# Padding a router's thin bf16 weights to 128 columns, and gating three token tiles at once

## The chip, the cores and the metric

The kernel runs on one core of one Trainium2 chip. The metric is the device time of the whole program in microseconds (us), as the median over runs.

## The reference, cut to what matters

Attention with random features gives 2304 token rows of 512. An MLP with a nonlinearity follows, and then a routed MLP with eight experts, in which the pairs of token and expert are taken in order of falling logit, and every expert takes 288 tokens.

```python
def _moe_ref(x, w_in, w_out):                  # 2304x512, 512x2048, 2048x512
    h = x @ w_in
    return (h - np.tanh(h)) @ w_out

def _moe2_ref(x, w_gate, w1, w2):              # w_gate 512x8, w1 8x512x1024, w2 8x1024x512
    cap = N // E                               # 288
    logits = x @ w_gate
    order = np.argsort(-logits.flatten())
    assigned = -np.ones(N); counts = np.zeros(E)
    for idx in order:
        tok, e = idx // E, idx % E
        if assigned[tok] >= 0 or counts[e] >= cap:
            continue
        assigned[tok] = e; counts[e] += 1
    for e in range(E):
        mask = assigned == e
        out[mask] = np.maximum(x[mask] @ w1[e], 0.0) @ w2[e]
```

## The kernel before, in words

Every operation is handed to a planner (`Plan`): it holds the operation's engine or engines, a planned duration, a due time (`plan.at` plus `lag`) and the buffers that it reads and writes. `Plan.run` deals out all operations in order of planned time and writes each engine's instructions in that order, which is fixed from then on. Loads and stores are issued by the SP queue (SyncE), also in a fixed order; a load whose buffer is not free holds everything behind it. A changed duration, buffer count or operation can shift the order of the operations after it.

The MLP works on six blocks (`j`) of 384 tokens, three tiles of 128 each. High and low parts of each operand are multiplied apart, three products for each pair (lines 603 to 605 for the first matrix, line 650 for the second). Blocks 0 to 3 end in `out_ops` and `gate_ops`, for each tile `t`: the output tile `xm` is transposed (line 672), copied into the buffer `mT`, of which there is one, and multiplied by `wg`, the gate's weights (line 676: the tile stands as 128 weight columns, `wg` moves with 8 columns, plain fp32, four products that appear as eight records). The logits go into `lg`. Blocks 4 and 5 run side by side and have their logits from `last_logits`. While they run, `low_ops` loads the first weight rows of the experts through the ring `dw` of four buffers (line 580), makes their low parts and stores them (line 587).

Then the experts are served one after another. For each expert but the last, `search_ops` finds the threshold logit digit by digit in seven steps. A step compares all logits with up to 32 thresholds on VectorE (`r_cmp`, line 1068), and counts on TensorE (line 1074): the stationary operand is `A2`, a bf16 tile of 18 token tiles x 32 columns of which 8 are in use, taken as 40 columns that span two token tiles, nine products for a step. VectorE turns the counts into a digit (`r_odd`, `r_cond`), TensorE spreads the digit to all partitions (line 1099, a bf16 operand of 128 columns), and VectorE makes the next thresholds. `route_ops` ranks the chosen tokens (lines 1163, 1164) and settles the capacities left (lines 1194 and 1195, weights of 8 columns). `place_ops` finds each slot's token in 18 products with weights of 32 columns (line 1231). `expert_ops` gathers the tokens and multiplies them with the expert's weights (lines 1380 to 1382 and 1399 to 1401, 288 tokens moving). The routing of the next experts stands among these products in TensorE's order.

`length_ops` (line 356) sums squares with bf16 weights of 128 columns and one moving column; it is not changed. `proj` (line 429) multiplies on two halves of the array's rows, plain fp32.

Of the kernel before, what the change touches and what calls it, by code (L numbers as in the profile page):

```python
# [8 lines left out]
F32 = mybir.dt.float32  # L9
F32R = mybir.dt.float32r  # L10
BF16 = mybir.dt.bfloat16
# [175 lines left out]
def tile_kernel(ctx, tc, q, k, v, omega, w_in, w_out, w_gate, w_gate_t, w1, w2, out, dbg=None):  # L187
# [56 lines left out]
    wg = consts.tile([P, NC, E], F32, name="wg")  # L244
# [51 lines left out]
    mTr = sring(wmid, [P, NC, P], F32, "mT", 1)  # L296
# [11 lines left out]

    bT = Buf(None)
# [355 lines left out]
    def gate_ops(j, t, xm):  # L665
        n = j * TPB + t
        tp, mT, lp = Buf(bank), Buf(mTr), Buf(bank)
        lgb = Buf(None)

        def transposes(e):  # L670
            for c in range(NC):
                nc.tensor.transpose(tp.t[:, c * P:(c + 1) * P], xm.t.bitcast(F32)[:, c * P:(c + 1) * P], ident)
# [5 lines left out]
        plan.op(PE, 0.44, transposes, r=[xm], w=[tp], lag=0.8)  # L678
        plan.op({ACT: 0.48, DVE: 0.6}, 0, lambda e: copy(e, mT.t.rearrange("p c n -> p (c n)"), tp.t), r=[tp], w=[mT],
                lag=1.5)  # L680
        plan.op(PE, 0.86, gate, r=[mT], w=[lp], lag=2.4)
        plan.op(DVE, 0.08, lambda e: nc.vector.tensor_copy(lg[:, n, :], lp.t[:, :E]), r=[lp], w=[lgb], lag=3.5)
# [63 lines left out]
    def mlp_ops(start, step, general=False):  # L746
# [4 lines left out]
        for j in range(NBLK - 1):  # L751
# [28 lines left out]
            if along and e1 == E:  # L780
                vg_split()
            for t in range(TPB):
                plan.at = start[j] + step[j] * NF + LAG2 + 0.7 * t
                xm, _ = out_ops(j, t, acc[t])
                gate_ops(j, t, xm)
# [141 lines left out]
    def r_setup():  # L927
# [20 lines left out]
        z = c.tile([P, n], I32, name="thr0s")  # L948
# [20 lines left out]
        sp = iota("spi", [P, P], [[0, P // LO], [1, LO]])  # L969
# [8 lines left out]
        t["tri"] = c.tile([P, P], BF16, name="tri")  # L978
        nc.vector.tensor_scalar(t["tri"], jp, 0.0, None, op0=OP.is_gt)
        t["ones"] = c.tile([P, P], BF16, name="onesb")  # L980
        nc.vector.memset(t["ones"], 1.0)
        t["one36"] = c.tile([P, 2 * NTT], F32, name="one36")
# [5 lines left out]
        t["mfull"] = c.tile([1, 1], BF16, name="mfull")  # L988
        nc.vector.memset(t["mfull"], -1.0e6)
# [29 lines left out]
    def best_ops(rS, after=()):  # L1019
# [9 lines left out]
        vec(0.22, lambda V: V.tensor_tensor(A2.t[:, :, :E], a.t, wide(am.t, E), op=OP.is_equal), r=[a, am], w=[A2])  # L1029
# [3 lines left out]
    pairs = []  # L1033
# [612 lines left out]
```

## Time and profile before

| | |
|---|---|
| median of 3 runs | 898.56 us (895.24 to 898.88) |
| the profiled execution | 897.55 us, of which 895.7 us lie between its first and its last instruction |
| TensorE, products | busy 863.1 us (96%), 6168 records |
| TensorE, weight loads | busy 768.8 us (86%) |
| VectorE | busy 657.8 us (73%) |
| ScalarE | busy 467.6 us (52%) |
| GpSimd | busy 252.5 us (28%) |
| mean granted TensorE clock | 0.988 of full speed |

Busy time counts an engine as busy from an instruction's start to its end, and instructions of TensorE overlap. [...]

### The profile page before, as it was taken

The page shows a single profiled execution, that of the slowest core. Times are in us where ns is not written, and L with a number is a line of the kernel's source. Part 1 is how long each engine was busy: PE and PEld are TensorE (multiplying, and loading weights), DVE is VectorE, ACT ScalarE, POOL GpSimd, SP SyncE. Part 2 cuts the span into 40 slices and gives each one's busy share as a digit, 9 for nine tenths or more (in the row PEclk, how much of TensorE's full clock was granted, in tenths as well). Part 3 has the DMA queues.
Part 4 walks back from the last instruction along what each step waited for, and adds up shares of the span by engine and source line. Part 5 has one row for each costly group of instructions (what it writes and reads, how often), then busy time and mean ns, then how long its engine had stood idle before and what let it go on. Part 6 is the DMA issues. An engine that isn't in the chain of part 4 may idle for free. (4 is left out here: it accounts for less than half of the span.)

```text
span 895.7 us, 17533 instructions
## 1 busy us (share of the span) xinstructions
PE 863.1 (96%) x6168; PEld 768.8 (86%) x6168; DVE 657.8 (73%) x1931; ACT 467.6 (52%) x1017; POOL 252.5 (28%) x272
## 2 busy tenths in 40 slices
PE   8988999999999999999999998989999999999995
PEld 6877888988989888889989995766999999999995
DVE  4998999777587879887867875445887887885520
ACT  4876564644456554655467771012465456465521
POOL 1122344143442435334520332010222322231211
PEclk8999999999999999999999999999999999999998
DMA  8988878877466665633478855576879878777600
GB/s 237 354 267 281 272 228 273 316 238 221 114 201 193 200 202 176 202 103 119 129 261 296 290 216 164 175 268 181 258 224 269 278 170 270 266 205 272 217 28 27
DMA packets 103789, 193.94 MB, mean 217 GB/s; under 512 B 28305, under 2 KB 42257, under 8 KB 103698
## 3 DMA queue, kind: packets, MB, share of 16 engines
q1 hardware_dynamic: 98034, 173.92, 59.3%
q0 software_dynamic: 5664, 18.88, 8.7%
q8 instruction: 49, 0.80, 0.4%
q14 instruction: 42, 0.34, 0.1%
HBM read 149.64 MB, written 33.69 MB: 205 GB/s over the span
## 5 line engine op out<-in xcount | busy, mean ns | idle before, releaser
L603 PE MATMUL bk<-xH,wi 128*128 128x384 f32 x332 | 118.3, 356 | 1.6 <-DVE xt L502 1.0
L604 PE MATMUL bk<-xL,wi 128*128 128x384 f32 x332 | 111.9, 337 | 0.5 <-DVE xL L305 0.5
L605 PE MATMUL bk<-xH,iL 128*128 128x384 f32 x332 | 112.1, 338 | 0.0
L650 PE MATMUL acc<-wo,gL 128*128 128x512 f32 x282 | 111.7, 396 | 0.0
L709 DVE SCALAR_TENSOR_TENSOR lw<-wf,raw 128x512 f32<-128x512 f32 x128 | 108.1, 844 | 2.2 <-POOL wf L706 1.0
L305 POOL TENSOR_TENSOR gL<-s,gH 128x384 fp32r<-128x384 f32 x51 | 61.0, 1196 | 138.3 <-ACT gH L300 128.9
L650 PE MATMUL acc<-wo,gH 128*128 128x512 f32 x240 | 99.8, 417 | 0.0
L440 ACT ACTIVATE phi<-bk,nm 128x128 f32<-128x128 f32 x272 | 77.0, 381 | 37.2 <-DVE nm L443 37.0
L650 PE MATMUL acc<-oL,gH 128*128 128x512 f32 x240 | 95.0, 396 | 0.3 <-DVE oL L305 0.3
L706 POOL TENSOR_TENSOR wf<-oL,wo 128x512 f32<-128x512 f32 x48 | 65.7, 1369 | 73.7 <-DMA oL<-low_wo 62.4
L300 ACT ACTIVATE gH<-s 128x384 fp32r<-128x384 f32 x80 | 42.1, 526 | 71.4 <-DVE s L630 48.5
L628 DVE SCALAR_TENSOR_TENSOR s<-s,bk 128x384 f32<-128x384 f32 x83 | 45.6, 550 | 37.1 <-ACT s L627 36.8
L603 PEld LDWEIGHTS bk<-xH,wi 128*128 128x128 f32 x332 | 62.9, 190 | 8.4 <-PE bk L482 1.3
L604 PEld LDWEIGHTS bk<-xL,wi 128*128 128x128 f32 x332 | 63.0, 190 | 3.3 <-DVE xL L305 0.7
L650 PEld LDWEIGHTS acc<-wo,gL 128*128 128x128 f32 x282 | 52.9, 188 | 12.6 <-POOL gL L305 0.3
L605 PEld LDWEIGHTS bk<-xH,iL 128*128 128x128 f32 x332 | 62.6, 189 | 0.0
L607 ACT ACTIVATE u<-bk 128x384 f32<-128x384 f32 x80 | 39.2, 489 | 39.8 <-PE bk L605 37.5
L443 DVE TENSOR_REDUCE nm<-bk 128x4 f32<-128x512 f32 (+1 forms) x75 | 46.4, 633 | 15.1 <-PE bk L429 14.1
L630 DVE SCALAR_TENSOR_TENSOR s<-s,u 128x384 f32<-128x384 f32 x80 | 54.6, 682 | 1.2
L650 PEld LDWEIGHTS acc<-wo,gH 128*128 128x128 f32 x240 | 45.2, 188 | 6.6 <-issue 0.2
L650 PEld LDWEIGHTS acc<-oL,gH 128*128 128x128 f32 x240 | 45.2, 188 | 6.5 <-DVE oL L305 1.0
L627 ACT ACTIVATE s<-u,qbias 128x384 f32<-128x384 f32 x80 | 49.2, 616 | 2.7 <-DVE gL L305 1.0
(402 smaller groups left out, 2347.0 us busy)
## 6 DMA issues: line engine op xcount, KB each, us to landing
r_wraw<-in_moe_w_dram SPq DMA_DIRECT2D x50, 512.0 KB, 6.0
iL<-low_wi SPq DMA_DIRECT2D x80, 256.0 KB, 3.3
oL<-low_wo SPq DMA_DIRECT2D x78, 256.0 KB, 2.7
raw<-in_moe_w_in_dram SPq DMA_DIRECT2D x32, 512.0 KB, 5.4
raw<-in_moe_w_out_dram SPq DMA_DIRECT2D x32, 512.0 KB, 4.2
dw<-in_moe_w_dram SPq DMA_DIRECT2D x16, 512.0 KB, 5.7
w1l<-dw SPq DMA_DIRECT2D x16, 512.0 KB, 3.0
s_wraw<-in_moe_w_dram SPq DMA_DIRECT2D x14, 512.0 KB, 5.6
```

The lines of the kernel that those rows point to most:

```text
L305: (nc.gpsimd if e == POOL else nc.vector).tensor_tensor(out, in_, high.bitcast(F32), op=OP.subtract)
L440: nc.scalar.activation(ph.t[:, i0 + i, :], pj.t[:, i * M:(i + 1) * M], AF.Exp, bias=nmx.t[:, i0 + i:i0 + i + 1])
L443: plan.op(DVE, 0.1 + 0.125 * n, lambda e, pj=pj, i0=i0, n=n: V.tensor_reduce(nmx.t[:, i0:i0 + n], pj.t[:, :n * M].rearrange("p (i m) -> p ...
L603: nc.tensor.matmul(ph(), piece(iH, c), xH.t[:, c, :], start=(c == 0), stop=False)
L604: nc.tensor.matmul(ph(), piece(iH, c), xL.t[:, c, :], start=False, stop=False)
L605: nc.tensor.matmul(ph(), piece(iL, c), xH.t[:, c, :], start=False, stop=(c == NC - 1))
L627: plan.op(ACT, 0.52, lambda e: nc.scalar.activation(s.t, ut(), AF.Square, bias=qbias), r=[u], w=[s], lag=2.8)
L628: plan.op(DVE, 0.52, lambda e: V.scalar_tensor_tensor(s.t, s.t, QD, ph(), op0=OP.add, op1=OP.mult), r=[p, s], w=[s], lag=3.4)
L630: plan.op(DVE, 0.65, lambda e: V.scalar_tensor_tensor(s.t, s.t, QC, ut(), op0=OP.mult, op1=OP.mult), r=[u, s], w=[s], lag=4.0)
L650: nc.tensor.matmul(acc[t].t, (gL if k == 2 else gH).t[:, c], (oL if k == 1 else oH).t, start=(f == 0 and k == 0), stop=(f == end and k == ...
L706: plan.op(POOL, 1.45, lambda e: nc.gpsimd.tensor_tensor(w.t, lo.t.bitcast(F32), wo[:, f, :].bitcast(F32), op=OP.add), r=[lo, wbuf["wo", f] ...
L709: x_reads.append(plan.op(DVE, 0.9, lambda e, i=i: nc.vector.scalar_tensor_tensor(scratch.t.bitcast(F32), w.t, 1.0, half(rows[i // 2], i % ...
```

## The change

Weights of the routing's thin products become 128 columns wide. In the counting products, 128 columns of `A2` are taken from column 32 j on, so each product reads the following token tiles too, whose counts land in partitions that nobody reads; `A2` (`pairs`) has two tiles more, which are zero. The placing products do the same with `lid`, which has three more zero tiles. The one-hot row `oh` and the sums `gs` are 128 wide with zeros behind the first eight columns, and `mfull` has 128 rows of which the first alone is not zero. These padded tiles are made once, with memsets on GpSimd.

The gate transposes and copies each tile as before, into an `mT` of 384 columns. Then one burst for the block takes `wg` (32 columns for each quarter of the model dimension, 8 in use, zeros behind) as the weights and the 384 tokens as the moving operand; the four quarters write to four column tiles of the array, 32 partitions each. The result is copied to `lT`, a buffer of the ring `s`, transposed back in three transposes, and VectorE sums the four quarters into `lg`.

To fit in memory, the ring `dw` has three buffers instead of four, and in the setup the tile `spi` takes the place of `jp` after `tri` has been made from it, and a scratch tile that of `one36`. The part of the program that only runs when the values are out of range (not in these runs) shares one more buffer and has other due times.

```diff
-    wg = consts.tile([P, NC, E], F32, name="wg")
+    wg = consts.tile([P, NC, P // NC], F32, name="wg")
-    mTr = sring(wmid, [P, NC, P], F32, "mT", 1)
+    mTr = sring(wmid, [P, NC, BLK], F32, "mT", 1)
...
-    def gate_ops(j, t, xm):
+    def gate_ops(j, xms):
+        mT, lp, lT, lgb = Buf(mTr), Buf(bank), Buf(sr), Buf(None)
+        own = lambda z, w: z.t[:, :TPB * w].rearrange("p (t n) -> p t n", t=TPB)
+        for t, xm in enumerate(xms):
+            tp = Buf(bank)
...
+            plan.op(PE, 0.44, transposes, r=[xm], w=[tp], lag=0.8 + 0.7 * t)
+            plan.op({ACT: 0.6, DVE: 0.68}, 0, lambda e, t=t, tp=tp: copy(
+                e, mT.t[:, :, t * P:(t + 1) * P], tp.t.rearrange("p (c n) -> p c n", n=P)), r=[tp], w=[mT], lag=1.5 + 0.7 * t)
         def gate(e):
             for c in range(NC):
-                nc.tensor.matmul(lp.t[:, :E], mT.t[:, c, :], wg[:, c, :], start=(c == 0), stop=(c == NC - 1))
+                nc.tensor.matmul(lp.t[c * P // NC:(c + 1) * P // NC, :BLK], wg[:, c, :], mT.t[:, c, :], start=True, stop=True,
+                                 skip_group_check=True)
+        def back(e):
+            for t in range(TPB):
+                nc.tensor.transpose(own(lp, P)[:, t, :], lT.t[:, t * P:(t + 1) * P], ident)
-        plan.op(PE, 0.86, gate, r=[mT], w=[lp], lag=2.4)
-        plan.op(DVE, 0.08, lambda e: nc.vector.tensor_copy(lg[:, n, :], lp.t[:, :E]), r=[lp], w=[lgb], lag=3.5)
+        plan.op(PE, 0.9, gate, r=[mT, bwg], w=[lp], lag=4.0)
+        plan.op({ACT: 0.48, DVE: 0.55}, 0, lambda e: copy(e, lT.t, lp.t[:, :BLK]), r=[lp], w=[lT], lag=5.0)
+        plan.op(PE, 0.33, back, r=[lT], w=[lp], lag=5.6)
+        plan.op(DVE, 0.25, lambda e: nc.vector.tensor_reduce(
+            lg[:, j * TPB:(j + 1) * TPB, :], own(lp, P).rearrange("p t (c e) -> p t e c", c=NC)[:, :, :E, :], axis=AX.X,
+            op=OP.add), r=[lp], w=[lgb], lag=6.0)
...
-        sp = iota("spi", [P, P], [[0, P // LO], [1, LO]])
+        t["tri"] = c.tile([P, P], BF16, name="tri")
+        nc.vector.tensor_scalar(t["tri"], jp, 0.0, None, op0=OP.is_gt)
+        sp = jp
+        nc.gpsimd.iota(sp, pattern=[[0, P // LO], [1, LO]], base=0, channel_multiplier=0)
...
-            t = wr[0].tile([P, NTT, 32], BF16, name=f"pairs{i}")
+            t = wr[0].tile([P, NTT + 2, 32], BF16, name=f"pairs{i}")
...
+            lids.append(Buf(None, wr[0].tile([P, NTT + 3, 2, LO], BF16, name=f"lid{i}")))
+            plan.op(POOL, 0.1, lambda e, i=i: nc.gpsimd.memset(lids[i].t[:, NTT:], 0.0), w=[lids[i]])
+        for n in ("oh", "gs"):
+            first[n] = Buf(None, wr[0].tile([P, P], BF16, name=n))
+            plan.op(POOL, 0.1, lambda e, n=n: nc.gpsimd.memset(first[n].t, 0.0), w=[first[n]])
...
-                        nc.tensor.matmul(cnt.t[:32 + E, :2 * n].rearrange("p (a n) -> p a n", a=2),
-                                         A2.t[:, j:j + 2].rearrange("p a e -> p (a e)")[:, :32 + E],
+                        nc.tensor.matmul(cnt.t[:, :2 * n].rearrange("p (a n) -> p a n", a=2),
+                                         A2.t[:, j:j + P // 32].rearrange("p a e -> p (a e)"),
                                          cmp.t[:, j - j0:j - j0 + 2, :n], start=(j == 0), stop=(j == NTT - 2))
...
-                nc.tensor.matmul(rp.t[:E, :1], gs.t, rt["ones"][:, :1], start=True, stop=False)
-                nc.tensor.matmul(rp.t[:E, :1], oh.t[0:1, :], rt["mfull"], start=False, stop=True)
+                nc.tensor.matmul(rp.t[:, :1], gs.t, rt["ones"][:, :1], start=True, stop=False)
+                nc.tensor.matmul(rp.t[:, :1], oh.t, rt["mfull"], start=False, stop=True)
...
-                nc.tensor.matmul(pi.t[:2 * LO, :NHI], lid.t[:, j].rearrange("p a l -> p (a l)"), ohh.t[:, j],
+                nc.tensor.matmul(pi.t[:, :NHI], lid.t[:, j:j + P // (2 * LO)].rearrange("p j a l -> p (j a l)"), ohh.t[:, j],
                                  start=(j == 0), stop=(j == NTT - 1))
...
-    plan.op(SP, 0.47, lambda e: nc.sync.dma_start(wg, w_gate.rearrange("(c p) e -> p c e", p=P)))
+    plan.op(POOL, 0.1, lambda e: nc.gpsimd.memset(wg, 0.0), w=[bwg])
+    plan.op(SP, 0.47, lambda e: nc.sync.dma_start(wg[:, :, :E], w_gate.rearrange("(c p) e -> p c e", p=P)), w=[bwg])
...
-        for r, n in zip(d_rings, (4, 2)):
+        for r, n in zip(d_rings, (3, 2)):
```

## Rows read from the trace of the kernel before

**Rows 1.** Busy time by stretch (us; instructions in brackets), clock, DMA share, GB/s.
```profile
core 0: us, PE busy (x) PEld busy (x) DVE busy (x) ACT busy (x) POOL busy (x), PEclk, DMA share, GB/s
200.00:265.00 65.00, 65.00 (x404) 57.87 (x404) 45.30 (x103) 33.48 (x81) 27.37 (x24) 1.00 0.60 176
476.00:548.00 72.00, 68.49 (x375) 60.97 (x375) 57.53 (x92) 48.92 (x98) 23.24 (x20) 0.98 0.68 242
660.00:694.00 34.00, 34.00 (x302) 31.44 (x301) 27.96 (x125) 19.21 (x32) 9.85 (x13) 1.00 0.94 271
```
**Rows 2.** Waits of TensorE from 548 us on: us in total, times, longest.
```profile
PE rp L1099 <- DVE r_cond L1095: 1.7, 3, 0.6
```
**Rows 3.** Timeline of TensorE in an expert phase: start, us, instruction, count.
```profile
647.51 0.29 PE L1382 MATMUL bd<-r_xgH,wi 128*128 128x288 f32 x1
647.73 0.44 PE L1074 MATMUL rp<-r_cmp,pairs 128*40 128x62 bf16 x9
...
648.34 0.30 PE L1381 MATMUL bd<-r_xgL,wi 128*128 128x288 f32 x1
...
648.89 0.29 PE L1401 MATMUL be<-s_hH,s_ewL 128*128 128x288 f32 x1
649.02 0.18 PE L1099 MATMUL rp<-id,d 128*128 128x8 bf16 x1
...
649.29 0.29 PE L1400 MATMUL be<-s_hL,wi 128*128 128x288 f32 x1
```
**Rows 4.** All counting and all digit products: duration min/median/max in ns, first and last start.
```profile
L1074 PE MATMUL rp<-r_cmp,pairs x441: 176/193/207, 550.1 to 793.3; 128*40 128x62 bf16 x84, 128*40 128x30 bf16 x42, 128*40 128x32 bf16 x21
L1099 PE MATMUL rp<-id,d x49: 166/180/183, 552.0 to 794.7; 128*128 128x8 bf16 x49
```
**Rows 5.** Timeline of TensorE, a count in two pieces.
```profile
555.42 0.29 PE L1074 MATMUL rp<-r_cmp,pairs 128*40 128x62 bf16 x4
```
**Rows 6.** Timeline of TensorE around a place burst.
```profile
672.90 0.30 PE L1382 MATMUL bd<-s_xgH,r_ewL 128*128 128x288 f32 x1
673.13 0.61 PE L1231 MATMUL rp<-r_ohh,r_lid 128*32 128x18 bf16 x18
...
673.91 0.29 PE L1381 MATMUL bd<-s_xgL,s_ewH 128*128 128x288 f32 x1
```
**Rows 7.** Timeline of TensorE around a settling pair.
```profile
667.16 0.29 PE L1382 MATMUL be<-s_xgH,s_ewL 128*128 128x288 f32 x1
667.39 0.17 PE L1194 MATMUL rp<-onesb,r_gs 128*8 128x1 bf16 x1
...
667.81 0.29 PE L1381 MATMUL be<-s_xgL,s_ewH 128*128 128x288 f32 x1
```
**Rows 8.** Timeline of TensorE in the MLP, around four bf16 products of 128 columns.
```profile
249.49 0.34 PE L605 MATMUL bk<-xH,iL 128*128 128x384 f32 x1
249.67 0.25 PE L356 MATMUL bk<-onev,sq 128*128 128x1 bf16 x4
...
250.04 0.34 PE L604 MATMUL bk<-xL,wi 128*128 128x384 f32 x1
```
**Rows 9.** Timeline of TensorE around one tile's gate products.
```profile
166.91 0.34 PE L605 MATMUL bk<-xH,iL 128*128 128x384 f32 x1
167.09 0.95 PE L676 MATMUL bk<-wg,mT 128*128 128x8 f32 x8
...
168.15 0.34 PE L604 MATMUL bk<-xL,wi 128*128 128x384 f32 x1
```
**Rows 10.** Timeline of TensorE: transposes of xm, then products on two row halves.
```profile
265.04 0.60 PE L672 MATMUL bk<-ident,xm 128*128 128x128 f32 x4
265.57 1.16 PE L429 MATMUL bk<-omT,ld 64*128 64x128 f32 x16
266.66 0.50 PE L650 MATMUL acc<-wo,gH 128*128 128x512 f32 x1
```
**Rows 11.** Loads and stores through dw: duration in ns, first and last start.
```profile
L580 SPq DMA_DIRECT2D dw<-in_moe_w_dram x16: 383/428/999, 447.9 to 524.8; - x16
L587 SPq DMA_DIRECT2D w1l<-dw x16: 337/338/423, 459.0 to 540.4; - x16
```

More of the change, by code (lines that the diff above doesn't have):

```diff
@@ L305, in low @@
         (nc.gpsimd if e == POOL else nc.vector).tensor_tensor(out, in_, high.bitcast(F32), op=OP.subtract)
+    bwg = Buf(None)
     bT = Buf(None)
@@ L663, in out_ops, with transposes @@
                            nbytes=P * DM * 4)
-    def gate_ops(j, t, xm):
[L666 to L672, printed above, removed]
+    def gate_ops(j, xms):
[3 more added lines that the diff above has]
+            tp = Buf(bank)
+            def transposes(e, tp=tp, xm=xm):
+                for c in range(NC):
+                    nc.tensor.transpose(tp.t[:, c * P:(c + 1) * P], xm.t.bitcast(F32)[:, c * P:(c + 1) * P], ident)
+            plan.op(PE, 0.44, transposes, r=[xm], w=[tp], lag=0.8 + 0.7 * t)
+            plan.op({ACT: 0.6, DVE: 0.68}, 0, lambda e, t=t, tp=tp: copy(
+                e, mT.t[:, :, t * P:(t + 1) * P], tp.t.rearrange("p (c n) -> p c n", n=P)), r=[tp], w=[mT], lag=1.5 + 0.7 * t)
@@ L781, in mlp_ops @@
                 vg_split()
+            xms = []
             for t in range(TPB):
                 plan.at = start[j] + step[j] * NF + LAG2 + 0.7 * t
-                xm, _ = out_ops(j, t, acc[t])
-                gate_ops(j, t, xm)
+                xms.append(out_ops(j, t, acc[t])[0])
+            plan.at = start[j] + step[j] * NF + LAG2
+            gate_ops(j, xms)
         j, lacc4, lprev4 = NBLK - 2, Buf(bank), None
@@ L947, in r_setup @@
         f0 = c.tile([P, n], I32, name="thr0")
-        z = c.tile([P, n], I32, name="thr0s")
+        t["one36"] = c.tile([P, 2 * NTT], F32, name="one36")
+        z = t["one36"].bitcast(I32)[:, :n]
         nc.vector.tensor_scalar(f0.bitcast(U32), x.bitcast(U32), 0x80000000, None, op0=OP.bitwise_xor)
@@ L987, in r_setup @@
         nc.vector.memset(t["asg"], 0.0)
-        t["mfull"] = c.tile([1, 1], BF16, name="mfull")
-        nc.vector.memset(t["mfull"], -1.0e6)
+        t["mfull"] = c.tile([P, 1], BF16, name="mfull")
+        nc.vector.memset(t["mfull"], 0.0)
+        nc.vector.memset(t["mfull"][:1], -1.0e6)
         t["id8"] = c.tile([P, E], BF16, name="id8")
@@ L1028, in best_ops @@
         vec(0.22, lambda V: V.tensor_reduce(am.t, a.t, axis=AX.X, op=OP.max), r=[a], w=[am])
-        vec(0.22, lambda V: V.tensor_tensor(A2.t[:, :, :E], a.t, wide(am.t, E), op=OP.is_equal), r=[a, am], w=[A2])
+        vec(0.22, lambda V: V.tensor_tensor(A2.t[:, :NTT, :E], a.t, wide(am.t, E), op=OP.is_equal), r=[a, am], w=[A2])
         return m, am, A2
-    pairs = []
+    pairs, lids = [], []
     def pairs_ops():
@@ L1144, in route_ops @@
         if not last:
-            oh, tie = tmp([P, E], BF16, "oh"), tmp([P, NTT], F32, "tie")
-            vec(0.14, lambda V: V.tensor_scalar(oh.t, w.t, mx.t, None, op0=OP.is_equal), r=[w, mx], w=[oh])
+            oh, tie = first["oh"], tmp([P, NTT], F32, "tie")
+            vec(0.14, lambda V: V.tensor_scalar(oh.t[:, :E], w.t, mx.t, None, op0=OP.is_equal), r=[w, mx], w=[oh])
             vec(0.22, lambda V: V.scalar_tensor_tensor(
-                S, oh.t[:, None, :].to_broadcast([P, NTT, E]), -BIG, S, op0=OP.mult, op1=OP.add), r=[oh, rS], w=[rS])
+                S, oh.t[:, None, :E].to_broadcast([P, NTT, E]), -BIG, S, op0=OP.mult, op1=OP.add), r=[oh, rS], w=[rS])
         vec(0.09, lambda V: V.tensor_tensor(av.t, gg.t[:, 1], flat(am.t), op=OP.mult), r=[gg, am], w=[av])
@@ L1181, in route_ops @@
             rp = Buf(rpr)
-            ga, gs = tmp([P, NTT, E], F32, "ga"), tmp([P, E], BF16, "gs")
-            vec(0.22, lambda V: V.tensor_tensor(ga.t, A2.t[:, :, :E], gg.t[:, 1].unsqueeze(2).to_broadcast([P, NTT, E]), op=OP.mult),
+            ga, gs = tmp([P, NTT, E], F32, "ga"), first["gs"]
+            vec(0.22, lambda V: V.tensor_tensor(ga.t, A2.t[:, :NTT, :E], gg.t[:, 1].unsqueeze(2).to_broadcast([P, NTT, E]), op=OP.mult),
                 r=[A2, gg], w=[ga], after=held if not p else later)
```

23 lines of the change are left out of this document (9 added, 14 removed).

## The prediction

> **What bounds the kernel now.** I read the windows by stage first. In the MLP and in the expert phases TensorE is busy for the whole stretch (65.00 of 65.00 and 34.00 of 34.00 us), while VectorE is at 45.3 of 65 and 28.0 of 34; only the stretch with blocks 4 and 5 together leaves 3.5 us of 72 free [rows 1]. The granted clock is 1.00 in two of the three stretches and 0.98 in the other, so the clock is no term of the sum. Busy TensorE is not TensorE at its peak, so the second view was the list of what TensorE waited for from 548 us on: the longest entry is 1.7 us in three waits for the routing's VectorE steps [rows 2]. So TensorE's own order of instructions sets the end almost everywhere, and what a product costs is the distance between starts, not its duration. That is the third view, the timeline of TensorE around single bursts. The reader is to see there how long the normal stream is interrupted.
>
> **The routing's thin products.** Normal pitch of the experts' products (288 moving columns) is 0.13 us (648.89 to 649.02) [rows 3]. I compare two interruptions, each from the last normal product before to the second normal one after, less two pitches (0.26). The digit product (L1099, bf16, 128 weight columns, one product): 649.29 - 648.89 = 0.40, so 0.14. The counting burst (L1074, bf16, 40 weight columns, nine products): 648.34 - 647.51 = 0.83, so 0.57 [rows 3]. Within the burst a product takes (0.44 - 0.193) / 8 = 0.03 [rows 3, 4]. Nine products at the price of the digit product's kind would cost 0.14 + 8 x 0.03 = 0.38. The remaining 0.19 is not work; it stands at the ends (the burst starts 0.22 after the product before it instead of 0.13, and the rest follows its last product). That four 128-wide bf16 products run without it is seen where the weights' squared lengths are summed (L356): 250.04 - 249.49 = 0.55 less two pitches of 0.18, so 0.19 for four, against 0.14 + 3 x 0.03 = 0.23 by the same rule [rows 8].
> The place products (L1231, 32 columns, 18 of them): 1.01 - 0.26 = 0.75 against 0.14 + 17 x 0.026 = 0.58, so 0.17 to gain [rows 6]; the pitch 0.026 is (0.61 - 0.17) / 17. The settling pair (L1194 and L1195, 8 columns): 0.65 - 0.26 = 0.39 against 0.14 + 0.03 = 0.17, so 0.22 [rows 7].
> Counts: 49 steps of the search (one digit product each [rows 4]) with nine counting products each (441). Seven steps come in two pieces, as in [rows 5], so 56 bursts: 56 x 0.2 = 11.2. Eight place bursts: 1.4. Seven settling pairs: 1.5. Together 14.1. In the steps where TensorE waits for VectorE already [rows 2], an earlier count brings nothing behind it; I take off 0.8. **Routing: -13.3 us** (bounds: 0 if width is not the cause; -14.1 as counted; for a gain beyond that every step would have to be in two pieces, which the timeline excludes).
>
> Against the change speaks that three times as many weight columns are loaded. The row to weigh is L356: the group of four lasts 0.25 where a single thin product lasts 0.17 [rows 7, 8], so 128-column loads follow each other by (0.25 - 0.17) / 3 = 0.027. So I cost the wider load at nothing. [...]
>
> **The gate logits.** Now every tile has a burst of eight records (four fp32 products) that costs 168.15 - 166.91 = 1.24 less two pitches of 0.18, so 0.88 [rows 9]; three tiles in a block 2.64, and four blocks have them. Afterwards a block has one burst of four products, 32 weight columns each and 384 moving, and three transposes back. Plain fp32 goes in two records for each product, and 16 records of 128 moving columns on two halves of the array take 1.09 us [rows 10]; less 0.19 for a switch that is 0.90, 0.11 for each pair if two run at once. Four transposes of that width take 0.53, 0.13 each, though each is one record [rows 10]; so two do run at once, and a record of 384 columns takes 3 x 0.11 = 0.33. All four column tiles at once: 2 x 0.33 = 0.66. None at once: 8 x 0.33 = 2.64. I take 1.0, near the lower end because the row halves of [rows 10] overlap, and not at it because one tile's two records are issued ahead of the next tile's. To it come 0.19 for the narrow weights and 0.42 (0.53 - 0.11) for three transposes: 1.61. **Gate: (2.64 - 1.61) x 4 = -4.1 us** (bounds -5.5 and +2.4). [...] The transposes of xm stay. The copies into mT stay too; new is one copy of 128 x 384 for each block on ScalarE or VectorE, and one reduction in place of three small copies. ScalarE has 31 us free of 65 there [rows 1]. They lengthen the way to lg, which the search first needs for its counts at 550 us [rows 4].
>
> **What pays for the memory.** The buffers of the expert weights' low parts (dw) go from four to three. First load to first store takes 459.0 - 447.9 = 11.1 us, and 16 loads to last store 92.5 [rows 11]. Sixteen turns of 11 to 14 us through three buffers take 59 to 75, which fits in 92.5. But a load that must wait for a buffer holds SP's queue, and behind it stand the loads of iL and oL that TensorE needs next. The least is nothing, the most I allow is that the stage's idle TensorE time of 3.5 us [rows 1] doubles. **+1.0** (0 to +3.5).
> The setup's second iota now overwrites jp, so GpSimd waits there for VectorE's tri; behind it on GpSimd stand the low parts gL, which TensorE needs. GpSimd is busy 27 of 65 us [rows 1] and catches up: **+0.3** (0 to +1). The GpSimd memsets of the padding come before the search and take the place of nothing TensorE waits for [rows 2]; the memset of wg stands ahead of its load far before its use: nothing, and at most a few tenths if SP stood behind it. Weights that are read over the neighbour's columns add rows of results that nobody reads. The planner's costs for the routing are the same, so that order stays; the MLP's order is dealt anew, which I allow 2 us either way.
>
> **Sum.** 897.55 (the profiled execution) - 13.3 - 4.1 + 1.0 + 0.3 = 881.5. The median of the runs is 1.0 above that execution; by the median it is 882.5. I say 882.
>
> **Rivals.**
> *Others become late.* When a stretch of 34 us loses seven counts, a place burst and a settling pair (1.8 us), VectorE's 28.0 us are 87% of it, and the DMA share, 0.94 in one phase, rises too [rows 1]. If half of the routing's gain turns into waits for r_cond, r_cmp or weights: 898.6 - 6.7 - 4.1 + 1.3 = 889. Against it: TensorE hardly waits for either today [rows 2]. 0.12.
> *The gate's tiles run one after another,* and the three dw buffers stall SP as well: 898.6 - 13.3 + 2.4 + 1 = 889. 0.05.
> *Width is not the cause.* If what costs 0.19 belongs to these bursts for another reason (say their bursts of accumulation), only the gate's gain is left: 898.6 - 4.1 + 1.3 = 896. Against it: L356 and L1099 are bf16 and accumulate or not, and neither pays it [rows 3, 8]. 0.06.
> *The other side: wide loads do not keep pace in long bursts.* L356 has four in a row; a burst of 9 or 18 could run at the load's own pace. The slowest row with 128-column weights and hardly any moving columns is the gate, 0.88 / 8 = 0.11 for a record [rows 9]. Then 441 x (0.11 - 0.03) + 144 x (0.11 - 0.026) = 47 us come back: 898.6 - 17.4 + 1.3 + 47 = 929. It decides from a pitch of about 0.057 on, where 585 x 0.028 eats the 16. Against it: the gate's weights are fp32, and the four bf16 loads show nothing of it [rows 8]. 0.05. [...]
>
> **How the numbers follow.** The forecast has 0.72. A change of 0.5% (4.5 us) is about what a measurement of this kernel can tell from none, so faster ends at 894. Forecast, late others and serial gate lie below it: 0.72 + 0.12 + 0.05 = 0.89. Width not the cause is the same: 0.06. Slow loads are slower: 0.05. The range goes down to 876 (routing -14.1, gate -5.5, order -2, no cost: 898.6 - 21.6 = 877, and one for the scatter of the runs) and up to 890, which takes in the second and third case. The forecast's own range is 877 to 887.
>
> **What would show it.** Right: counting bursts that start 0.13 after the normal product before them and total about 0.38; each expert's phase shorter by about 1.8 us, so the end moves step by step from 550 us on; gate bursts of about 1 us, four of them; VectorE's busy share up and TensorE's waits still short. Wrong: a pitch inside the counts above 0.05; waits for r_cond in most steps; idle TensorE between 450 and 545 us behind SP's dw loads; a gate burst of 2.5 us.

## The result, and the profile after it

The changed kernel takes 887.11 us (median of 4 runs, 885.15 to 888.42) beside 898.72 (4 runs of the kernel before in the same session, 895.24 to 903.1): a ratio of 0.9865 [0.9839, 0.9892]. It is faster by 11.6 us, 1.3%. The forecast was 16. The profiled execution took 886.79 us, with a span of 884.9 and a mean clock of 0.984.

First the burst that carried most of the forecast. TensorE's timeline of the changed kernel around one counting burst, one settling pair and one place burst (start, us, instruction, count):

```profile
643.20 0.29 PE L1423 MATMUL be<-s_hH,s_ewL 128*128 128x288 f32 x1
643.34 0.44 PE L1096 MATMUL rp<-r_cmp,pairs 128*128 128x62 bf16 x9
643.61 0.38 PE L1421 MATMUL be<-s_hH,s_ewH 128*128 128x288 f32 x1
643.83 0.29 PE L1422 MATMUL be<-s_hL,s_ewH 128*128 128x288 f32 x1
...
661.99 0.29 PE L1404 MATMUL be<-s_xgH,s_ewL 128*128 128x288 f32 x1
662.12 0.18 PE L1216 MATMUL rp<-onesb,gs 128*128 128x1 bf16 x1
...
662.41 0.29 PE L1403 MATMUL be<-s_xgL,s_ewH 128*128 128x288 f32 x1
...
666.61 0.30 PE L1423 MATMUL be<-s_hH,wi 128*128 128x288 f32 x1
666.75 0.61 PE L1253 MATMUL rp<-r_ohh,lid 128*128 128x18 bf16 x18
...
667.43 0.29 PE L1422 MATMUL be<-s_hL,wi 128*128 128x288 f32 x1
```

Read as the prediction read them: from the last normal product before to the second normal one after, less two pitches (0.26). Counts: 643.83 - 643.20 = 0.63, so 0.37 (0.57 before [rows 3], 0.38 forecast). Settling pair: 0.42, so 0.16 (0.39 before [rows 7], 0.17 forecast). Place: 0.82, so 0.56 (0.75 before [rows 6], 0.58 forecast). The burst starts 0.14 after the product ahead of it, no longer 0.22. Each burst got shorter by what was forecast.

The gate's burst in the same timeline, and the three transposes back:

```profile
172.80 0.33 PE L606 MATMUL bk<-xH,iL 128*128 128x384 f32 x1
173.06 0.85 PE L682 MATMUL bk<-mT,wg 128*32 128x384 f32 x8
173.84 0.66 PE L553 MATMUL bk<-ident,xt 128*128 128x128 f32 x4
...
176.40 0.39 PE L651 MATMUL acc<-wo,gL 128*128 128x512 f32 x1
176.63 0.49 PE L687 MATMUL bk<-ident,s 128*128 128x128 f32 x3
176.96 1.04 PE L553 MATMUL bk<-ident,xt 128*128 128x128 f32 x8
```

The eight records of four products start in two groups of four, 0.007 us apart within a group and 0.33 between the groups (173.060, 173.067, 173.073, 173.080, then 173.407 to 173.427), and each record lasts 0.49 to 0.51: all four column tiles run at once. The burst costs 173.84 - 172.80 less one pitch of 0.17, which is 0.87; the transposes 0.33. That is 1.2 for a block where 1.61 was forecast.

Then what TensorE waits for in the changed kernel, first from 530 us on, then within the six phases from expert 1's first product to expert 7's (653 to 847 us) (us in total, times, longest; waits under 0.15 us are not listed):

```profile
PE acc L651 <- SPq L1530: 3.9, 1, 3.9
PE bd L1369 <- DMA r_xg<-ms,r_ix: 2.7, 2, 1.9
PE rp L1121 <- DVE r_cond L1117: 2.6, 3, 1.4
...
PE rp L1121 <- DVE r_cond L1117: 1.4, 1, 1.4
PE be L1364 <- DMA r_xg<-ms,r_ig: 1.3, 2, 1.1
PE be L1364 <- DMA xg_rest<-ms,r_ig: 0.7, 2, 0.6
PE rp L1253 <- DVE r_ohh L1247: 0.4, 1, 0.4
```

Before, the longest waits from 548 us on were three for r_cond, 1.7 us together [rows 2], and the same view of the six phases (662 to 858 us) had no entry at all. So waits have appeared that were not there. The windows by stage (us, busy time of PE, PEld, DVE, ACT and POOL with instructions, clock, DMA share, GB/s) show the same:

```profile
476.00:548.00 72.00, 66.34 (x355) 57.84 (x354) 52.27 (x92) 43.99 (x88) 23.50 (x25) 0.93 0.69 240
532.00:548.00 16.00, 10.50 (x44) 7.54 (x43) 5.74 (x23) 1.89 (x4) 2.53 (x8) 0.68 0.52 182
660.00:694.00 34.00, 34.00 (x322) 32.42 (x321) 28.26 (x134) 18.50 (x31) 9.09 (x12) 1.00 0.84 245
694.00:728.00 34.00, 32.28 (x307) 30.44 (x307) 27.49 (x128) 17.75 (x29) 9.71 (x12) 1.00 0.81 233
```

One phase is full as before [rows 1], the next is short of 1.7 us, and the stretch with blocks 4 and 5 now holds 5.7 us of idle TensorE and a granted clock of 0.93. The largest single wait is at the branch that separates the MLP from the experts (L1530), where TensorE waits for SP's queue for 3.93 us and GpSimd for 8.81. TensorE and SP around it:

```profile
534.70 0.47 PE L651 MATMUL acc<-wo,wi 128*128 128x512 f32 x1 [1.33 <-PEq L1530]
539.09 0.79 PE L651 MATMUL acc<-xm,wi 128*128 128x512 f32 x1 [3.93 <-SPq L1530]
539.68 0.63 PE L651 MATMUL acc<-wo,gLk 128*128 128x512 f32 x1
540.11 0.63 PE L651 MATMUL acc<-wo,wi 128*128 128x512 f32 x1
```
```profile
535.05 0.34 SPq L588 DMA_DIRECT2D w1l<-dw  x1
539.93 0.34 SPq L855 DMA_DIRECT2D gL<-g4l  x1
```

SP reaches the branch only after its last store from dw, at 535.05, and TensorE gets on 4.04 us later. After that idle time its products start 0.43 apart instead of 0.23: the granted clock is 0.50 of full speed from 535.1 to 545.3 us (0.53 in the window from 535 to 536 us, 0.50 from 536 to 545, 0.85 from 545 to 546).

Five stretches, each taken from the first product of its stage, show where the time went in the kernels of this study (us, worked out from one profiled execution of each; "gate" runs from block 0's first product to block 4's, "blocks 4, 5" to the first of the MLP's last products, which stand around the branch, "branch" to the first count, "expert 0" to expert 1's first product, "experts" to expert 7's; the rest is 38.4 to 38.8 everywhere). Two borders need care. "Gate" holds the gate bursts of three blocks; the fourth's stand behind block 4's first product. And the wait at the branch falls into "branch" in most kernels, but into "blocks 4, 5" in e6_store_act, e7_both and e9_e1_ties, while the border of e2_dw3_only lies 1.9 us ahead of its branch; so these two columns are best read as a sum. The order column is explained with the experiments.

| kernel | order | gate | blocks 4, 5 | branch | expert 0 | experts |
|---|---|---|---|---|---|---|
| before | 1 | 388.8 | 103.9 | 4.5 | 112.2 | 195.0 |
| after | 2 | 384.6 | 97.8 | 9.3 | 109.1 | 193.4 |
| e1_routing_only | 3 | 388.5 | 104.0 | 4.4 | 109.8 | 188.1 |
| e2_dw3_only | 4 | 389.6 | 95.8 | 12.2 | 114.4 | 195.0 |
| e3_gate_only | 2 | 382.9 | 97.8 | 9.0 | 111.1 | 198.9 |
| e4_dw_early | 2 | 384.9 | 97.8 | 8.8 | 108.2 | 194.1 |
| e5_order | 1 | 385.3 | 97.7 | 9.3 | 113.3 | 192.2 |
| e6_store_act | 2 | 385.6 | 99.6 | 4.3 | 110.2 | 197.1 |
| e7_both | 1 | 383.3 | 99.6 | 4.5 | 111.6 | 191.5 |
| e8_counts96 | 2 | 385.6 | 97.8 | 8.8 | 111.7 | 197.3 |
| e9_e1_ties | 3 | 385.8 | 99.7 | 4.5 | 110.9 | 188.4 |
| e10_before_ties | 2 | 389.3 | 104.1 | 4.5 | 111.1 | 197.5 |
| e11_after_e1_ties | 3 | 383.4 | 97.8 | 8.9 | 110.1 | 189.4 |
| e12_counts64 | 2 | 384.5 | 97.7 | 9.4 | 115.0 | 198.1 |

The time ahead of block 0 lies between 50.7 and 55.1 us without regard to the kernel; it is scatter. The experiments ran in three sessions, in which the kernel before took 896.79 (e1 to e4), 900.8 (e5 to e8) and 898.89 us (e9 to e12), so ratios are to be compared, and times only within a session.

### The profile page after: what moved, and what is told of

Read it like the earlier page. It is cut to its first block, busy times and chain, and to the rows that moved or that the text cites. A ratio compares the mean times of both kernels' runs of the same rounds, so it can differ in the third digit from the quotient of the medians.

```text
span 884.9 us, 17420 instructions
## 1 busy us (share of the span) xinstructions
PE 846.3 (96%) x6116; PEld 756.0 (85%) x6116; DVE 654.1 (74%) x1925; ACT 470.2 (53%) x1021; POOL 252.9 (29%) x276
## 5 line engine op out<-in xcount | busy, mean ns | idle before, releaser
L305 POOL TENSOR_TENSOR gL<-s,gH 128x384 fp32r<-128x384 f32 x49 | 58.1, 1186 | 138.4 <-ACT gH L300 138.4
L651 PEld LDWEIGHTS acc<-wo,gL 128*128 128x128 f32 x282 | 53.3, 189 | 12.2
L444 DVE TENSOR_REDUCE nm<-bk 128x4 f32<-128x512 f32 (+1 forms) x75 | 46.3, 632 | 12.2 <-PE bk L430 11.1
```

The source lines that it names most:

```text
L305: (nc.gpsimd if e == POOL else nc.vector).tensor_tensor(out, in_, high.bitcast(F32), op=OP.subtract)
L444: plan.op(DVE, 0.1 + 0.125 * n, lambda e, pj=pj, i0=i0, n=n: V.tensor_reduce(nmx.t[:, i0:i0 + n], pj.t[:, :n * M].rearrange("p (i m) -> p ...
L651: nc.tensor.matmul(acc[t].t, (gL if k == 2 else gH).t[:, c], (oL if k == 1 else oH).t, start=(f == 0 and k == 0), stop=(f == end and k == ...
```

## The experiments

**The three parts alone.** The first kernel is the changed one with the gate and the four dw buffers of before; the second is the kernel before with three dw buffers; the third is the changed one with the routing's narrow products of before.

```diff
 e1_routing_only, against the changed kernel
-    def gate_ops(j, xms):
+    def gate_ops(j, t, xm):
...
-        for r, n in zip(d_rings, (3, 2)):
+        for r, n in zip(d_rings, (4, 2)):
 e2_dw3_only, against the kernel before
-        for r, n in zip(d_rings, (4, 2)):
+        for r, n in zip(d_rings, (3, 2)):
 e3_gate_only, against the changed kernel
-                        nc.tensor.matmul(cnt.t[:, :2 * n].rearrange("p (a n) -> p a n", a=2),
-                                         A2.t[:, j:j + P // 32].rearrange("p a e -> p (a e)"),
+                        nc.tensor.matmul(cnt.t[:32 + E, :2 * n].rearrange("p (a n) -> p a n", a=2),
+                                         A2.t[:, j:j + 2].rearrange("p a e -> p (a e)")[:, :32 + E],
...
```

> Only the routing's weights are widened; the gate is that of before and dw has four buffers, so the MLP up to 545 us should be that of before. Theory A (each narrow bf16 burst pays about 0.2 us on TensorE at its ends, 13 us in all, and part of it comes back as waits of TensorE for gathered rows and routing steps of VectorE): about 890 us (887 to 893), bursts of nine counts at 0.34 to 0.38 as in the changed kernel, 6 to 9 us won between 550 us and the end. Rival B (the routing's part is all given back to waits, and the whole gain of the changed kernel is the MLP's, which reaches its end 11 us earlier): 896 to 899 us.

Measured: 0.9909 [0.9879, 0.9939], 888.42 us. Its two stages before the branch stand as before; expert 0 takes 2.4 us less and the experts 6.9 less. The width is the cause of the shorter bursts (0.36 for a burst of nine, as in the changed kernel), and this kernel alone has most of the gain, as theory A expected. It also got an order of its own behind the branch, order 3, in which narrow products were never run; how much of the 6.9 is the order's is not shown.

> The kernel before with three dw buffers instead of four, nothing else. Theory A (with three buffers the last store of the low parts is issued so late that SP reaches the branch after the MLP as the last engine, and TensorE's second product after it waits some 4 us at half clock): 2 to 6 us slower than before, 901 to 905 us, with such a wait near 545 us. Rival B (SP's lateness in the changed kernel comes from its MLP ending earlier than the store stream, whatever the buffers; three buffers cost nothing here): 898 to 900 us.

Measured: 0.9999 [0.9974, 1.0024], 897.32 us. The time stayed, as rival B expected, but not because nothing happened: the wait of theory A is there. Up to the branch, blocks 4 and 5 take 6.2 us less (97.7 beside 103.9), and from the branch to the first count it takes 5.8 us more. TensorE's timeline of this kernel there, and SP's last store:

```profile
542.33 0.47 PE L650 MATMUL acc<-wo,wi 128*128 128x512 f32 x1 [0.57 <-PEq L1507]
547.68 0.79 PE L650 MATMUL acc<-xm,wi 128*128 128x512 f32 x1 [4.88 <-SPq L1507]
```
```profile
543.63 0.34 SPq L587 DMA_DIRECT2D w1l<-dw  x1
```

So the wait comes with the three buffers, but not because they make the stores late. Counted from block 4's first product, the last store goes out after 98.7 us with four buffers and after 99.0 with three (98.1 to 99.0 in all 14 kernels). What moved is TensorE. Before, it reached the branch 5.2 us after the last store (545.60 and 540.38), and nothing was left to wait for; here it is there ahead of the store and gets on 4.05 after it. The time saved ahead of the branch is handed over to the wait. Where the 6.2 come from is not settled: TensorE's same 553 products of that stretch stand in another order here, and its idle time fell from 5.4 to 1.7 us; the granted clock, 0.50 from 463.8 to 467.2 us in the kernel before, is 1.00 in that stretch of the changed kernel (437 to 535 us), which is 6.1 us shorter; no run parts the buffers from the order.

> Only the new gate (with three dw buffers and the setup's shared tiles); the routing's weights stay 40, 32 and 8 columns wide. Theory A (four column tiles at once save 1.3 us for each of four blocks, the end of blocks 4 and 5 waits less, SP's late store takes 4 to 5 us back): 892 to 896 us, with the MLP's end about 11 us earlier as in the changed kernel. Rival B (the MLP's gain is not the gate's but an accident of the order dealt anew together with the routing's operations): MLP end within 4 us of before and 897 to 900 us.

Measured: 0.9997 [0.9965, 1.0028], 895.42 us. The time lies in theory A's range, but only because the kernel before took 896.79 beside it; the ratio shows no gain. In the profiled execution the gate's stage gains 5.9 us and blocks 4 and 5 6.1, and most of it is spent again: 4.5 at the branch and 3.9 among the experts, whose products this kernel doesn't change at all. That last loss was the riddle. Its order of instructions behind the branch is the same as that of the changed kernel, and another than before.

**The wait at the branch.** The loads and stores through dw get earlier due times; or the last two stores go through ScalarE's queue; ScalarE has little to do there (in the changed kernel it is busy 1.89 of the 16 us from 532 to 548 us).

```diff
 e4_dw_early, against the changed kernel
-    low_ops(starts[-2], (NF * steps[-1] + 4.0) / (E * NPRE))
+    low_ops(starts[-2], (NF * steps[-1] - 8.0) / (E * NPRE))
 e6_store_act, against the changed kernel
-            plan.op(SP, 0.47, lambda e, raw=raw, e_=e_, r=r: nc.sync.dma_start(w1l[e_, r, :], raw.t), r=[raw],
-                    nbytes=P * n * 4, lag=6.8)
+            plan.op(SP if k < E * NPRE - 2 else ACT, 0.47, lambda e, raw=raw, e_=e_, r=r: (
+                nc.sync if e == SP else nc.scalar).dma_start(w1l[e_, r, :], raw.t), r=[raw], nbytes=P * n * 4, lag=6.8)
```

> The changed kernel with the due times of the dw loads packed closer, so that the last of 16 is due 11 us earlier. Theory A (the 4.2 us wait of TensorE after the branch and the half clock of 10 us behind it come from the last low-part store on SP): the wait near 535 us shrinks below 1 us and the time falls to 881 to 885 us. Rival B (SP waits there for something else, or the crowd of transfers earlier in blocks 4 and 5 costs as much): 886 to 890 us.

Measured: 0.9895 [0.985, 0.9939], 887.24 us. The wait stayed at 3.93 us, and the last store went out at 536.56, which is 98.1 us after block 4's first product, as in the changed kernel. So the edit did not move the stores at all and decides nothing about the wait; that the planner holds each load back until a store has freed one of the three buffers is the likely reason, not a tested one.

> The changed kernel with the last two stores of low parts issued from ScalarE's queue instead of SP's. Theory A (TensorE's 4.2 us wait after the branch comes from SP, which stands behind the last store and reaches the branch last): the wait falls below 1.5 us, the half-clock stretch behind it gets shorter, 882 to 885 us. Rival B (whoever holds the last store, the branch is late, for instance since ScalarE is now the last): the wait stays and the time is 886 to 889 us.

Measured: 0.9855 [0.9835, 0.9875], 888.09 us. The time is rival B's, and the wait did not fall below 1.5 us: it moved to ScalarE's queue.

```profile
PE acc L651 <- ACTq L1530: 3.1, 1, 3.1
```

But TensorE now gets on 1.5 us after the last store (535.10, then 536.56) and not 4.0, so blocks 4 and 5 and the branch together took 103.9 instead of 107.1; the granted clock from 532 to 548 us was 0.89 instead of 0.68 (by estimate 3.5 us at 0.50 instead of 10.2), and the first count came 3.1 us sooner. What takes the other 2.5 us when SP issues the last store is not shown. Then the experts took 197.1, 3.7 more than in the changed kernel, and the gain was gone. The same order gave 193.4, 194.1 and 197.1 in three kernels with wide products: its waits for gathered rows and VectorE differ, and with one profile of each it is open whether by kernel or by execution.

**The order behind the branch.** The planner gives out operations by the key `(round(t / 0.03), o.prio)`: planned starts that fall into the same step of 0.03 are a tie. At the branch all engines' planned times are set to one value, `now`, and that value depends on the costs of everything before. Apart from a few short memsets on GpSimd the operations behind the branch and their costs are the same in both kernels; `now` differs, so ties round otherwise, and 603 of TensorE's 953 operations there get another place. Adding less than 0.04 to `now` chooses between orders without touching an operation. Four orders appeared: 1 is that of the kernel before, 2 that of the changed kernel, 3 that of e1_routing_only, 4 that of e2_dw3_only. The five kernels that choose an order:

```diff
 e5_order, against the changed kernel (e7_both has the stores of e6_store_act as well)
-    now = max(plan.free.values())
+    now = max(plan.free.values()) + 0.03854
 e11_after_e1_ties, against the changed kernel (e9_e1_ties has the stores of e6_store_act as well)
+    now = max(plan.free.values()) + 0.03669
 e10_before_ties, against the kernel before
+    now = max(plan.free.values()) + 0.02146
```

> The changed kernel with one number added: the planner's clock at the start of the routing stage is moved by 0.03854 us of planned time, so that its ties (times are compared in steps of 0.03) fall as in the run with the routing's weights alone; no operation is changed. Theory A (in the changed kernel the order of routing and experts was dealt anew by those ties, and the new order lets TensorE wait for gathered rows and for VectorE): the stretch from the second to the last expert, 193.4 us now, falls to 187 to 190, and the whole time to 881 to 885 us. Rival B (the waits are what faster TensorE runs into in any order): within 1.5 us of the changed kernel, 885.5 to 888.5 us.

Measured: 0.987 [0.9845, 0.9895], 888.84 us. The order that it writes is not that of e1_routing_only, as was meant, but that of the kernel before, which makes it the better test: it is the order that the prediction counted on. The time is the changed kernel's (0.9865), so theory A's gain did not come. The experts take 192.2, only 2.8 less than with narrow products in the same order, and expert 0 takes 1.1 more. The waits of its TensorE among the experts, where the kernel before has none:

```profile
PE rp L1121 <- DVE r_cond L1117: 3.4, 6, 0.9
```

Here the first rival of the prediction is seen as it was described: with the bursts shorter, VectorE's digit is late in steps where it was in time before.

> Both of the two edits before. Theory A: the two add up, 877 to 881 us. Rival B: neither or one alone, 882 to 888 us.

Measured: 0.9823 [0.9801, 0.9845], 884.44 us, in rival B's range and short of theory A's. Blocks 4 and 5 and the branch together take 104.1 instead of 107.0, and with this order the program keeps that gain.

> The kernel before with the planner's clock at the start of the routing stage moved by 0.02146 us, with which every engine's order behind the branch is exactly that of the changed kernel; no operation is changed. Theory A (the order dealt anew costs some 4 us by itself, as the run with the gate alone, 198.9 us from the second to the last expert against 195.0, suggests): 197.5 to 200 us for this stretch, ratio 1.002 to 1.007. Rival B (the order is worth nothing, the gate's run lost its 3.9 us otherwise): 194 to 196 us, ratio 0.998 to 1.002.

Measured: 1.0008 [0.9985, 1.0032], 900.43 us. With narrow products, order 2 costs the experts 2.4 us and gives expert 0 1.1 back. The experts stand at the lower edge of theory A's range, the ratio in rival B's: in the time of the whole program no loss can be told from none.

> The changed kernel with the last two low-part stores from ScalarE's queue and the planner's clock at the start of the routing stage moved by 0.03669 us, with which every engine's order behind the branch is exactly that of the run with the routing's weights alone. Theory A (that order is the better one, 188.1 us from the second to the last expert, and the gate's and the store's gains come on top): 187 to 190 us for this stretch and a ratio to before of 0.974 to 0.980. Rival B (the 188.1 us was one execution's luck with transfers): 191 to 194 us and 0.981 to 0.986.

Measured: 0.9822 [0.9789, 0.9856], 881.8 us (877.56 to 888.58). The experts took 188.4, as theory A expected, but the ratio is rival B's: the gains did not add up in full.

> The changed kernel with the planner's clock moved by 0.03669 us alone, the stores as they are. Theory A: the better order without the earlier branch, 187 to 190 us from the second to the last expert, TensorE's 4.2 us wait after the branch stays, ratio 0.979 to 0.984. Rival B: as the changed kernel, 0.985 to 0.988.

Measured: 0.9827 [0.9796, 0.9858], 884.58 us, as theory A expected, the wait of 4.0 included. The changed kernel in order 3 needs 189.4 for the experts instead of 193.4. The same view of the experts, first e9_e1_ties (651 to 840 us), which has one wait where the changed kernel has six, then both kernels' windows, the changed kernel first:

```profile
PE rp L1096 <- DVE r_cmp L1090: 0.8, 1, 0.8
```
```profile
653.08:846.49 193.41, 189.43 (x1724) 181.78 (x1723) 146.18 (x645) 104.86 (x174) 50.52 (x67) 1.00 0.78 239
```
```profile
651.49:839.88 188.39, 187.57 (x1714) 181.33 (x1713) 144.24 (x628) 106.07 (x175) 48.41 (x67) 1.00 0.80 246
```

The idle time falls from 4.0 us to 0.8, at the same clock. Kernels e7, e9 and e11 are the fastest of the study, about 1.8% below the kernel before. Their intervals and that of the changed kernel still touch, so that they beat it is likely, not settled. And since narrow products never ran in order 3, it is open whether this order is better in itself or only for wide products. The stores on ScalarE's queue add nothing that shows in order 3 (0.9822 beside 0.9827).

**Why a narrow burst costs more.** Only the counts change, to 96 and to 64 columns; place and settling stay at 128. Each of the two kernels was timed once.

```diff
 e8_counts96 (e12_counts64 has 64 and j + 2), against the changed kernel
-                        nc.tensor.matmul(cnt.t[:, :2 * n].rearrange("p (a n) -> p a n", a=2),
-                                         A2.t[:, j:j + P // 32].rearrange("p a e -> p (a e)"),
+                        nc.tensor.matmul(cnt.t[:96, :2 * n].rearrange("p (a n) -> p a n", a=2),
+                                         A2.t[:, j:j + 3].rearrange("p a e -> p (a e)"),
```

> The changed kernel with the counting products alone at 96 weight columns instead of 128, with the same results. Theory A (what is paid at the ends of a burst goes away at the full width of 128 only): a burst of nine costs 0.55 to 0.6 us beside the normal pitch again, 8 to 11 us slower than the changed kernel, about 896 us. Rival B (the price falls with the columns, or two rows of column tiles suffice): 0.35 to 0.45 for a burst of nine, 886 to 890 us.

> The changed kernel with the counting products at 64 weight columns. After the run with 96 there are two prices: one at the ends of a burst, which 96 did not pay, and one for each product, 0.045 us at 96 instead of 0.029 at 40 and 0.028 at 128. [...] Rival B' (the first goes away with any width over 40): 0.33 to 0.40 us for a burst of nine, start 0.13 after the product before.

Measured: 893.49 us with 96 columns (before: 900.8 on the same chip) and 898.66 with 64 (before: 898.89). TensorE's timeline, 96 columns first, then 64:

```profile
641.68 0.30 PE L1404 MATMUL bd<-r_xgH,wi 128*128 128x288 f32 x1
641.82 0.55 PE L1096 MATMUL rp<-r_cmp,pairs 128*96 128x62 bf16 x9
642.21 0.38 PE L1421 MATMUL be<-s_hH,wi 128*128 128x288 f32 x1
642.43 0.30 PE L1422 MATMUL be<-s_hL,wi 128*128 128x288 f32 x1
```
```profile
671.39 0.29 PE L1404 MATMUL bd<-s_xgH,s_ewL 128*128 128x288 f32 x1
671.61 0.47 PE L1096 MATMUL rp<-r_cmp,pairs 128*64 128x62 bf16 x9
672.01 0.40 PE L1402 MATMUL bd<-s_xgH,s_ewH 128*128 128x288 f32 x1
672.25 0.29 PE L1403 MATMUL bd<-s_xgL,s_ewH 128*128 128x288 f32 x1
```

With 96 columns a burst costs 0.47, which neither expectation had: more than rival B's, less than theory A's, and without a price at the ends. With 64 it costs 0.59, far above rival B''s range, and starts 0.22 after the product ahead. So there are two prices, one at the burst's ends and one for each product. Medians over the nine-product bursts among the experts' products (28 before, 20 in each of the others; us):

| columns | start after the product ahead | pitch inside | last count to second product after | burst, less two pitches |
|---|---|---|---|---|
| 40 | 0.224 | 0.031 | 0.358 | 0.560 |
| 64 | 0.224 | 0.034 | 0.361 | 0.592 |
| 96 | 0.131 | 0.043 | 0.261 | 0.469 |
| 128 | 0.136 | 0.030 | 0.244 | 0.357 |

The price at the ends (0.09 ahead, 0.10 to 0.11 behind) is full at 40 and 64 columns and nought at 96 and 128. The pitch is low at 40, 64 and 128 and higher at 96. So an account in which only exactly 128 columns escape the end price falls: 96 do too. With 64 columns the bursts are as dear as before and nothing of the counts' gain is left: counted from block 0 on, that execution is 10.6 us longer than the changed kernel's, beside 49 x (0.592 - 0.357) = 11.5 from the table.

Why the ends cost at 40 and 64 columns and not at 96 and 128 no row shows; here it is 0.2 us for each burst. For the second column there are the weight loads' own records: they last 98, 113, 125 and 98 ns at 40, 64, 96 and 128 columns (medians of 441 in each kernel). At 96, where the pitch is highest, the load is longest too, and at 128 it is as short as at 40; why is not shown either.

## Why the prediction was right, and where it was not

The time lies in the predicted range, 5 us above the forecast, and the change is faster, as forecast. That is in part luck: 887.11 is at the very end of the forecast's own range (877 to 887), and the range reaches to 890 because of two rivals that were given 0.17 together, of which the first has the mechanism that was seen. Step by step (us; from the two profiled executions):

| term | forecast | found |
|---|---|---|
| bursts of the routing on TensorE | -14.1 | -13.0 |
| gate, blocks 0 to 3 | -4.1 | -4.1 (three of the four bursts) |
| dw with three buffers (blocks 4, 5 and branch) | +1.0 | -1.4 (with the fourth burst) |
| setup, start | +0.3 | -0.6 |
| what waits give back | +0.8 | +8.4 |
| sum | -16.1 | -10.8 |

*The bursts: right in mechanism and size.* The 13.0 is the excess of all distances between starts over the normal pitch, waits above 0.25 left out: 11.4 to 5.4 us up to expert 1, and 15.4 to 8.4 from there to expert 7. The rivals that width is not the cause and that wide loads don't keep pace are out: the first by e1_routing_only and by the return of the price at 64 columns, the second by the pitch of 0.030 at 128 columns in the table above and 0.025 among the place products.

*The gate: right, a little better on TensorE.* The burst and its transposes cost 1.2 for a block and not 1.61, which makes (2.64 - 1.2) x 4 = 5.8. The stage up to block 4's first product holds three of the four, 4.3; it became 4.1 shorter here, 5.9 in e3_gate_only. The prediction's 1.0 for the burst lay between all four tiles at once (0.66) and none; all at once was the case.

*dw: next to nothing, as the least forecast had it, but not by the path forecast.* The prediction had a dw load that waits for a buffer hold back the loads behind it within blocks 4 and 5. Instead blocks 4 and 5 took 6.1 us less, of which the fourth gate burst is 1.4; for the MLP's order dealt anew the prediction had allowed only 2 us either way. TensorE then reached the branch ahead of the last store: 4.8 us more from the branch to the first count, of which the wait is 3.9; the rest goes with the granted clock of 0.50, which lasts 10.2 us there instead of 3.4. The store stream itself was no later. Together the two sides cost nothing, as e2_dw3_only confirms. The -0.6 of the setup is less than the scatter of the time ahead of block 0.

*What waits give back: the step that failed.* The prediction took off 0.8, because TensorE hardly waited for VectorE before [rows 2]. Found were 8.4: 13.0 saved on bursts, of which 3.0 arrive as a shorter expert 0 and 1.6 as shorter experts. Most of it can be seen between the first count and expert 7's first product: TensorE's waits of 0.15 us and more add up to 8.7 us instead of 3.8, and 4.8 us pass at a granted clock of 0.50 (544.0 to 545.3 and 589.7 to 593.1 us), which by estimate costs 2.4 (before, the clock is 1.00 throughout, 550.1 to 857.3 us). The remaining 1.1 is not accounted for.
- The step was to take short waits for slack. That is the first rival's mechanism, to which the prediction gave 0.12, and its 889 is nearer to the 887 measured than the forecast's 882. In order 1, the one that the prediction counted on, wide products in e5_order save 2.8 of 7 us among the experts and nothing in expert 0, and the six waits for r_cond stand where there were none. What in the profile spoke for it was there: VectorE at 28.0 of 34 us in a phase [rows 1]. What spoke against it, short waits, says how much slack there is at the present pace only as "not yet negative", and not how much.
- The prediction also held that the planner's order stays since the routing's costs do. It did not: equal costs are not enough for an equal order where ties are rounded on absolute planned time. But this is not what cost the forecast its gain: put back into order 1, the changed kernel takes as long (0.987 beside 0.9865), and the kernel before in order 2 loses nothing that can be told from none (1.0008). What other orders show is that some of the gain could be had: wide products gave 188 to 189 us for the experts in order 3, 191 to 192 in order 1 and 193 to 197 in order 2.

In expert 0's stretch bursts saved 6.0 and 3.0 arrived. The granted clock of 0.50 took by estimate 2.4 of the rest, 0.7 of it behind the branch and 1.7 behind waits for gathered rows, which grew from 1.6 to 2.7 us. Before, they were these two:

```profile
PE bd L1347 <- DMA r_xg<-ms,r_ix: 0.9, 1, 0.9
PE bd L1347 <- DMA xg_rest<-ms,r_ix: 0.7, 1, 0.7
```

What stays open: how much of the difference between orders comes from the places of the gathers and how much from the digit's steps; the runs show the waits, not one of them removed by itself. Open too is why three buffers shorten blocks 4 and 5. And the spread of order 2 with wide products (193.4 to 197.1) was seen in single profiles.

## What to carry to other kernels

Read the price of a thin product from starts, between the last product before and the second after: here a narrow bf16 burst cost 0.2 us at its ends that no duration shows, and with weights of 96 and 128 columns it was gone, at 128 without a dearer pitch (0.030 us beside 0.031 at 40). Before counting saved time as won, ask of each follower how much slack it has, and not only whether it waits today. In a kernel whose order comes out of a planner, try a few orders that differ by ties alone before judging a change: going from order 2 to 3 shortened the experts by 4.0 and 8.7 us in single profiles, and the whole program by about 3 us, with intervals that touch.

## What was not expected of the hardware

Not every narrow product pays. Fp32 products with 16 and 8 weight columns stand among normal ones without an end price: in e2_dw3_only such a product starts 0.174 after a normal one of 384 columns, and a normal one 0.173 after such a product (medians of 23 and 28). TensorE's timeline of that kernel shows an 8-column product between others, each start 0.17 to 0.18 after the one before, which is the pitch of 384 moving columns, and the one behind it 0.23 after, the pitch of 512:

```profile
540.08 0.34 PE L721 MATMUL kv<-gH,vgs 128*16 128x384 f32 x1
540.25 0.34 PE L723 MATMUL kv<-gL,vgs 128*8 128x384 f32 x1
540.43 0.39 PE L650 MATMUL acc<-wo,wi 128*128 128x512 f32 x1
540.66 0.40 PE L650 MATMUL acc<-oL,wi 128*128 128x512 f32 x1
```

The gate's fp32 burst of 32 columns starts 0.26 after its neighbour, 0.09 more than a pitch, so it pays at its head. Which of the two a narrow product does was not settled; no run varied these products' widths.

With the wait came a lower granted clock. In the changed kernel TensorE idled 1.33 and 3.93 us around a single product; the clock was 0.50 from 535.1 us on, and the products behind the wait started 0.43 apart until 545.3 us: 6.2 us at 0.50, so by estimate 3.1 us lost. In the kernel before it is 0.50 behind the branch as well, from 545.7 to 549.1 us, 1.7 us lost by the same estimate; so the change added 1.4. In e9_e1_ties, with 3.33 us of idle time, the mean of the window from 532 to 548 us is 0.89, where it is 0.68 in the changed kernel; by estimate a clock of 0.50 lasted (1 - 0.89) x 16 x 2 = 3.5 us in all, as long as before. That the idle time brings the lower clock no run shows. The window in e9_e1_ties:

```profile
532.00:548.00 16.00, 12.36 (x64) 8.90 (x65) 6.88 (x27) 1.58 (x4) 2.53 (x8) 0.89 0.61 198
```
